# Sliding-window attention and a two-layer MLP on one core: the attention of batches 2 to 7 in blocks of 64 queries and 128 keys

## The chip, the core and the metric

The kernel runs on one core of a Trainium2 chip. A core has a matmul engine (PE, TensorE), three engines for elementwise work (DVE, VectorE; ACT, ScalarE; POOL, GpSimd) and an engine that issues most transfers (SP, SyncE). They run side by side and wait for each other by semaphores; each works through its own instructions in order. Sixteen DMA engines move data. Matmuls write to PSUM, which has eight banks of 512 float32 columns per partition; everything else lies in SBUF. The metric is the time of one execution on the device in microseconds (us).

## The reference

There are 8 batches, 8 heads, 576 tokens and a head dimension of 64. Each query attends to keys at most 32 positions away. The result, 4608 tokens of 512 values, goes through two layers (512 to 2048 to 512) with a leaky ReLU between.

```python
scores = scale * np.matmul(q, k.transpose(0, 1, 3, 2))
mask = np.abs(pos[:, None] - pos[None, :]) <= window      # window = 32
scores = np.where(mask, scores, -1000000000.0)
attn = np.exp(scores - max); attn = attn / (sum + 1e-09)
x = np.matmul(attn, v)          # then (B, S, H*D)
h = x @ w_in; g = np.maximum(0.01 * h, h); out = g @ w_out
```

The kernel leaves the maximum out: the scores are small, so exp is taken directly, masked entries are multiplied by 0, and the products are divided by the sum of the exponentials.

## The kernel before

**Tiling.** Two heads make a pair, which fills the 128 partitions (2 x 64); there are four pairs. The attention of a half batch (288 queries) and one pair is a *chunk*: 8 chunks a batch, 64 in all. The first layer works by *groups* of 288 tokens, 16 of them; for each, `h_tile` makes 16 tiles of 128 hidden units from four matmuls of 288 columns (L348), and ACT evicts each with the leaky ReLU (L355). The second layer works by 36 output tiles of 128 tokens, each 16 matmuls of 512 columns (L390), evicted by ACT (L395) and stored by SP (L396).

**A chunk.** `score` multiplies five block-diagonal key blocks (`kbd`: 64 keys of each head, zeros in the other head's quarter) by windows of queries (L275). Keys 64 at a time with a window of 32 each side reach up to 128 queries, so the five blocks overlap and the scores go to two layers of 288 columns. ACT takes the exponential of 576 columns (L280), POOL multiplies by a mask (L282) into `prob`. `join` adds the two layers on DVE (L292); `sums` multiplies the result by a block of ones, so that each column's sum stands on all 64 rows of its head (L301), and DVE takes the reciprocal (L309). `product` multiplies five block-diagonal value blocks (`vbd`) by `prob` (L320), and DVE's multiply by the reciprocal (L334) writes the columns of `xT`, the first layer's input.

**Getting batches in.** For batches 0 and 1 PE transposes queries and keys (`transposes`, L225). For batches 2 to 7 SP loads q and k in pieces of 512 bytes (L81), POOL casts them to bfloat16, two copies for each (L197), SP issues one DMA transpose each for q and k (`transpose_dma`, L212), and two DVE copies put the keys into `kbd` (`place_keys`, L260). Two tokens lie side by side in a piece, so tokens stand even and odd apart all the way, and the eviction L355 puts them back in order. Values are loaded by head (L91) and cast by POOL into `vbd` (L205; batch 1's by ACT, L203).

**Order.** The order of work on each engine is that of the program. `step()` does one chunk's share: the join of the next chunk, the score of the chunk after the next, sums, product and scaling of this one, placements, casts and loads by tables of due steps (`qk_due`, `v_due`). At the end of the program a list `plan` holds the matmuls of both layers, tile after tile; `spend` walks a clock along it and calls `step()` when the next chunk is due. A group's last chunk is due 4 us (`LEAD`) of the plan's time ahead of its first layer. Batch 0, and the start of batch 1, are written out by hand before that.

**Buffers.** `xT` and `gT` (the hidden units) are rings of 1152 tokens. PSUM has four banks for both layers (`mm`), two for the scores (one set), and one each for `x` and `s`.

Of the kernel before, what the change touches and what calls it, by code (L numbers as in the profile page):

```python
# [16 lines left out]
def kernel(  # L17
# [38 lines left out]
    outp = ctx.enter_context(tc.tile_pool(name="outp", bufs=4))  # L56
# [11 lines left out]
    def load_qk(b, p, behind=None):  # L68
# [3 lines left out]
        for into, src, name in ((qf, q, "qf"), (kf, k, "kf")):  # L72
# [5 lines left out]
            if b < BY_DMA:  # L78
                nc.sync.dma_start(out=t, in_=heads.rearrange("a (p c) d -> p a (c d)", c=RUN))
            else:  # L80
                nc.sync.dma_start(  # L81
                    out=t.rearrange("p a (g e) -> p a g e", g=3),
                    in_=heads.rearrange("a (g p c) d -> p a g (c d)", g=3, c=2),
                )
            into[b, p] = t

    def load_v(b, p):

        t = fload.tile([128, NB, D], FP32, name=f"vf{p}")
# [5 lines left out]
        vf[b, p] = t  # L95
# [24 lines left out]
    kbd = [const.tile([128, NPAIR, NB, 128], BF16, name=f"kbd{i}") for i in range(2)]  # L120
    vbd = [const.tile([128, NPAIR, NB, 128], BF16, name=f"vbd{i}") for i in range(2)]
# [12 lines left out]
    nc.vector.memset(kbd[0], 0.0)  # L134
# [31 lines left out]

    NPROB = 6
# [10 lines left out]
    RING = 4 * HALF  # L178
    xT = const.tile([128, NPAIR, RING], BF16)
# [4 lines left out]
    qT = {}  # L184

    def cast_qk(b, p, q_eng=None):
        for eng, src, dst in ((q_eng or nc.gpsimd, qf, qb), (nc.gpsimd, kf, kb)):
            if b < BY_DMA:
                parts = [(dst[:, p], src[b, p].rearrange("p a (c d) -> p c a d", d=D))]
            else:  # L190
                by_c = src[b, p].rearrange("p a (g c d) -> c p g a d", g=3, c=2)
                parts = [(dst[:, p, 3 * c:3 * c + 3], by_c[c]) for c in range(2)]
            for to, tok in parts:
                if eng is nc.scalar:
                    eng.activation(out=to, in_=tok, func=AF.Copy)
                else:
                    eng.tensor_copy(out=to, in_=tok)  # L197
# [8 lines left out]

    def transpose_dma(b, p):
        if b not in qT:
            qT[b] = attn.tile([128, NPAIR, S], BF16, name="qT")
        kT = kt.tile([128, S], BF16, name="kT")  # L210
        for t, src in ((qT[b][:, p], qb), (kT, kb)):
            nc.sync.dma_start_transpose(  # L212
                out=t.rearrange("p (c i) -> p c i", c=RUN),
                in_=src[:, p].rearrange("p c a d -> p (c a d)"),
            )
        landing.append((8 * (b - 1) + 4 + p, b, p, kT))

    def transposes(b):

        qT[b] = attn.tile([128, NPAIR, S], BF16, name="qT")  # L220
# [27 lines left out]
    def place_keys():  # L248

        while landing and landing[0][0] <= state["done"]:  # L250
            unplaced.append(landing.pop(0)[1:])
        while unplaced:
            b, p, kT = unplaced.pop(0)
            for a in range(2):
                r = slice(64 * a, 64 * a + 64)
                to = kbd[b % 2][r, p, :, r]
                if b < BY_DMA:
                    nc.vector.tensor_copy(out=to, in_=kT[r].rearrange("p (n j) -> p n j", j=64))  # L258
                else:
                    nc.vector.tensor_copy(  # L260
                        out=to.rearrange("p n (m c) -> p n c m", c=2),
                        in_=kT[r].rearrange("p (c n m) -> p n c m", c=2, n=NB),
                    )
# [5 lines left out]

    def score(i):  # L270
        b, hf, p = where(i)
# [23 lines left out]
    def sums(i):  # L295
# [3 lines left out]
        s = xps.tile([128, HALF], FP32, name="s")  # L299
# [12 lines left out]
    def product(i):  # L312
# [3 lines left out]
        x = xps.tile([128, HALF], FP32, name="x")  # L316
# [19 lines left out]
    def weighted(i):  # L336
        if probs[i][2] is None:
            sums(i)
# [6 lines left out]

    def h_mms(g, f, h, cs):
        for c in cs:
            nc.tensor.matmul(  # L348
                h[:, 0:HALF], w_in_bf[:, c, ts(f, 128)], xT[:, c, ds(g * HALF % RING, HALF)],
# [3 lines left out]
    def h_out(g, f, h):  # L353

        nc.scalar.activation(  # L355
            out=gT[:, f, ds(g * HALF % RING, HALF)].rearrange("p (i c) -> p i c", c=2),
# [293 lines left out]
```

## Time and profile before

| | |
|---|---|
| median of three runs | 320.09 us (319.89 to 320.62) |
| span of the profiled execution | 318.99 us |
| PE busy, 0 to 53 us | 39.37 us |
| PE busy, 53 to 122 us | 68.55 of 69 us |
| PE busy, 122 to 250 us | 127.53 of 128 us |
| first layer, L348 | 1024 matmuls of 288 columns |
| second layer, L390 | 16 matmuls for each of 36 tiles |
| reciprocal L309, DVE | 64 times 1956 ns |
| mask L282, POOL | 64 times 1276 ns |
| exp L280, ACT | 64 times 648 ns |
| eviction L355, ACT | 256 times 412 ns |
| waits of DVE's reciprocal on PE's sums L301 | 53.3 us in all |

A row of a group of instructions gives the busy time and the mean of one. Busy times of matmuls overlap, since one starts before the former has left the array; the time that a matmul takes in a row of others is read from start to start. The profiled execution is one of its own, so its span differs a little from the median of the runs. Idle time of an engine that is not the one that sets the end costs nothing.

### The profile page before, as it was taken

To read this page: it belongs to the slowest core of one execution; us is meant where nothing else is said; L and a number is where in the kernel's file an instruction comes from. 1 tells how busy PE (TensorE), PEld (TensorE's weight loads), DVE (VectorE), ACT (ScalarE), POOL (GpSimd) and SP (SyncE) were. 2 spreads that over 40 slices of the span, in tenths; PEclk is the share of its full clock that TensorE was granted. 3 is DMA by queue.
4 is the path that set the end of the run, shared out by engine and by line. 5 is a ranking of instruction groups with operands and counts; after the bars stand their busy time and mean duration, and the time that the engine had idled before them with its cause. 6 is when DMAs were issued, how large, how long until landed. Compare 5 with 4: busy or idle time off the path is not lost.

```text
span 319.0 us, 6455 instructions
## 1 busy us (share of the span) xinstructions
PE 301.1 (94%) x2429; PEld 203.5 (64%) x2449; DVE 220.7 (69%) x258; ACT 183.5 (58%) x394; POOL 191.2 (60%) x251
## 2 busy tenths in 40 slices
PE   2678998999999999999999999999999999999996
PEld 1457764576765858576765858576665858576653
DVE  5688886869755987688755987688745988565100
ACT  7686688574652828375552828465552837464531
POOL 7899963974646866585646866586637866330000
PEclk9999999999999999999999999999999999999999
DMA  8999998997998989399835996399833440000102
GB/s 189 224 184 229 269 242 188 242 200 180 223 245 167 245 148 210 79 237 202 173 76 114 233 229 151 74 215 223 178 76 104 108 71 33 35 35 2 66 31 71
DMA packets 108400, 49.46 MB, mean 155 GB/s; under 512 B 68816, under 2 KB 103888, under 8 KB 108368
## 3 DMA queue, kind: packets, MB, share of 16 engines
q1 hardware_dynamic: 104144, 44.84, 66.0%
q0 software_dynamic: 4224, 4.19, 8.1%
q8 instruction: 19, 0.31, 0.5%
q14 instruction: 13, 0.11, 0.1%
HBM read 36.70 MB, written 9.44 MB: 145 GB/s over the span
## 4 chain that ended last, share of the span: by engine, by line
PE 88%; DVE 5%; ACT 3%; issue 2%; POOL 1%; ACTq 0%; POOLq 0%; DVEq 0%
PE mm L390 38%; PE mm L348 37%; PE x L320 5%; PE ps L275 5%; PE s L301 2%; DVE r L309 2%; DVE qb L197 1%; PE s L304 1%; DVE kbd L258 1%; POOL prob L282 1%; ACT kT L239 1%; PE tp L225 1%; ACT e L280 1%; ACT vbd L203 1%; DVE kbd L134 1%
## 5 line engine op out<-in xcount | busy, mean ns | idle before, releaser
L309 DVE RECIPROCAL r<-s 128x288 f32<-128x288 f32 x64 | 125.2, 1956 | 57.0 <-PE s L301 53.3
L282 POOL TENSOR_TENSOR prob<-e,mask 128x576 bf16<-128x576 bf16 x64 | 81.6, 1276 | 89.2 <-ACT e L280 42.1
L348 PE MATMUL mm<-xT,w_in_bf 128*128 128x288 bf16 x1024 | 134.0, 286 | 0.1
L390 PE MATMUL mm<-w_out_bf,gT 128*128 128x512 bf16 (+2 forms) x572 | 128.7, 373 | 1.1
L355 ACT ACTIVATE gT<-mm 128x288 bf16<-128x288 f32 x256 | 101.2, 412 | 25.6 <-PE mm L348 9.1
L348 PEld LDWEIGHTS <-w_in_bf 128*128 128x128 bf16 x1024 | 98.4, 98 | 24.5 <-issue 0.3
L390 PEld LDWEIGHTS <-gT 128*128 128x128 bf16 x592 | 56.3, 98 | 59.2
L395 ACT ACTIVATE o_sb<-mm 128x512 f32<-128x512 f32 (+2 forms) x37 | 21.7, 585 | 91.8 <-PE mm L390 89.0
L280 ACT ACTIVATE e<-ps 128x576 bf16<-128x576 f32 x64 | 41.5, 648 | 10.6 <-PE ps L275 10.5
L197 POOL CAST kb<-kf 96x384 bf16<-96x384 f32 (+1 forms) x56 | 34.8, 643 | 4.5 <-DMA kf<-in_k_dram 4.3
L205 POOL CAST vbd<-vf 64x576 bf16<-64x576 f32 x50 | 34.7, 694 | 1.5
L334 DVE TENSOR_TENSOR xT<-x,r 128x288 bf16<-128x288 f32 x64 | 29.2, 457 | 7.8 <-PE x L320 1.1
L260 DVE COPY kbd<-kT 64x576 bf16<-64x576 bf16 x48 | 32.3, 674 | 0.6 <-DMA kT<-kb 0.3
L320 PE MATMUL x<-prob,vbd 128*128 128x128 bf16 (+2 forms) x320 | 26.0, 213 | 2.7 <-ACT vbd L203 1.3
L275 PEld LDWEIGHTS <-kbd 128*128 128x128 bf16 x320 | 20.8, 99 | 10.7 <-DVE kbd L258 1.6
L275 PE MATMUL ps<-qT,kbd 128*128 128x128 bf16 (+2 forms) x320 | 26.3, 214 | 1.3 <-DVE kbd L258 0.8
L197 POOL CAST qb<-qf 96x384 bf16<-96x384 f32 x48 | 24.4, 536 | 0.0
L320 PEld LDWEIGHTS <-vbd 128*128 128x128 bf16 x320 | 20.5, 99 | 5.4 <-ACT vbd L203 1.9
L292 DVE TENSOR_TENSOR both<-prob 128x288 bf16<-128x288 bf16 x52 | 20.0, 384 | 0.9
L301 PE MATMUL s<-both,ones_bd 128*128 128x288 bf16 x52 | 14.9, 286 | 0.0
L258 DVE COPY kbd<-kT 64x576 bf16<-64x576 bf16 x16 | 7.1, 446 | 6.2 <-ACT kT L239 6.0
L225 PE MATMUL tp<-ident,qb 96*128 96x96 bf16 x48 | 4.1, 233 | 6.8 <-DVE qb L197 6.8
(43 smaller groups left out, 87.9 us busy)
## 6 DMA issues: line engine op xcount, KB each, us to landing
qf<-in_q_dram SPq DMA_DIRECT2D x32, 288.0 KB, 4.6
kf<-in_k_dram SPq DMA_DIRECT2D x32, 288.0 KB, 5.3
vf<-in_v_dram SPq DMA_DIRECT2D x64, 144.0 KB, 4.4
out_dram<-o_sb SPq DMA_DIRECT2D x35, 256.0 KB, 3.9
w_in_bf<-in_moe_w_in_dram POOLq DMA_DIRECT2D x4, 512.0 KB, 8.2
w_out_bf<-in_moe_w_out_dram POOLq DMA_DIRECT2D x4, 512.0 KB, 16.4
qT<-qb SPq DMA_TRANSPOSE x24, 4.2
kT<-kb SPq DMA_TRANSPOSE x24, 3.1
```

The costliest lines, as they stand in the source:

```text
L197: eng.tensor_copy(out=to, in_=tok)
L205: nc.gpsimd.tensor_copy(out=vbd[b % 2][r, p, :, r], in_=vf[b, p][r])
L260: nc.vector.tensor_copy(out=to.rearrange("p n (m c) -> p n c m", c=2), in_=kT[r].rearrange("p (c n m) -> p n c m", c=2, n=NB),)
L275: nc.tensor.matmul(ps_v[:, n_, :, i0:i0 + n], kbd[b % 2][:, p, blk], by_c[:, :, hf * EVEN + i0:hf * EVEN + i0 + n], start=True, stop=True,)
L280: nc.scalar.activation(out=e, in_=ps[:, P0:P0 + 2 * HALF], func=AF.Exp, scale=scale)
L282: nc.gpsimd.tensor_mul(pr.rearrange("p n c i -> p (n c i)"), e, mask[hf].rearrange("p n c i -> p (n c i)"),)
L309: nc.vector.reciprocal(r, s)
L320: nc.tensor.matmul(x_v[:, :, i0:i0 + n], vbd[b % 2][:, p, blk, :], pr[:, n_, :, i0:i0 + n], start=(blk == parts[0][1]), stop=(blk == parts ...
L334: nc.vector.tensor_mul(place(i), x, r)
L348: nc.tensor.matmul(h[:, 0:HALF], w_in_bf[:, c, ts(f, 128)], xT[:, c, ds(g * HALF % RING, HALF)], start=(c == 0), stop=(c == DMC - 1),)
L355: nc.scalar.activation(out=gT[:, f, ds(g * HALF % RING, HALF)].rearrange("p (i c) -> p i c", c=2), in_=h[:, 0:HALF].rearrange("p (c i) -> ...
L390: nc.tensor.matmul(o[:, lo:hi], gT[:, f, ds(128 * j % RING, 128)], w_out_bf[:, f, lo:hi], start=(f == 0), stop=(f == FFC - 1),)
```

## The change

Batches 0 and 1 are computed as they were. From batch 2 on:

- The 54 blocks of 64 queries (9 a batch) are numbered through. A chunk is four of them (256 queries) and one pair; it may span two batches. There are 14 x 4 = 56 such chunks, the last four with two blocks each.
- A score is one matmul for each block (L354): 128 keys as weights (64 and 32 on each side, `kz`, padded with zeros at the ends of a batch) and 2 x 64 columns of queries, which stand in `qz` once for each head, with zeros on the other head's rows. Exp and mask are over 512 columns; the mask is one band (`band`). The score bank alternates between two.
- A product is two matmuls for each block (L372), one a head, of 64 columns. Its weights are the head's 64 value columns beside 64 columns of ones (`vw`: values, ones, values), so the product and the sum of the exponentials come out of one matmul. `join` and `sums` are gone there. The sums stand on the other head's partitions: two ACT copies bring them over (L379, L380), then come the reciprocal in SBUF (L381) and two multiplies (L385). `x` alternates between two banks.
- q and k are loaded in pieces of 256 bytes, with tokens in order; POOL casts each in one copy. The DMA transpose writes keys straight into `kz`; the two DVE copies are now of the queries, into `qz` (`place_queries`, L298). Values are loaded for two pairs by five transfers in 128-token windows offset by 32 and cast by three POOL copies (`cast_vw`).
- The first layer works by groups of 256, 256, five times 512, and 384 tokens; the rings are used to 1024 tokens. The due steps come from a table of how many chunks each group needs, with a lead of 5 us.
- `qT`, `kbd` and `vbd` share two large tiles with `qz`, `kz` and `vw`, so zeros and ones are written anew by DVE while batches 0 and 1 run (`clear_q`, `ready`, called through `chore`). There are three output buffers instead of four.

```diff
+    def score_blocks(i):
+        p, bs = i % NPAIR, blocks_of(i)
+        n = 2 * 64 * len(bs)
+        lo = 512 * (i % 2)
+        sc = ps[:, lo:lo + n].rearrange("p (a w i) -> p a w i", a=2, i=64)
+        for w, (b, m) in enumerate(bs):
+            nc.tensor.matmul(
+                sc[:, :, w], kz[b % 2][:, p, 64 * m:64 * m + 128],
+                qz[b % 2][:, p, :, 64 * m:64 * m + 64], start=True, stop=True,
+            )
+        e = attn.tile([128, 2 * HALF], BF16, name="e")
+        nc.scalar.activation(out=e[:, 0:n], in_=ps[:, lo:lo + n], func=AF.Exp, scale=scale)
+        pr = prob[:, i % NPROB].rearrange("p n c i -> p (n c i)")[:, 0:n]
+        nc.gpsimd.tensor_mul(pr, e[:, 0:n], band.rearrange("p w i -> p (w i)")[:, 0:n])
...
+    def product_blocks(i):
...
+        x = xps.tile([128, 512], FP32, name="xs"[i % 2])
+        x = x[:, 0:2 * n].rearrange("p (a w i) -> p a w i", a=2, i=64)
+        for a in range(2):
+            for w, (b, m) in enumerate(bs):
+                nc.tensor.matmul(
+                    x[:, a, w],
+                    vw[b % 2][:, p, m, a:a + 2].rearrange("p n d -> p (n d)"),
+                    pr[:, a, w], start=True, stop=True,
+                )
+        x = x.rearrange("p a w i -> p a (w i)")
+        r = recip.tile([128, HALF], FP32, name="r")
+        nc.scalar.activation(out=r[0:64, 0:n], in_=x[64:128, 0], func=AF.Copy)
+        nc.scalar.activation(out=r[64:128, 0:n], in_=x[0:64, 1], func=AF.Copy)
+        nc.vector.reciprocal(r[:, 0:n], r[:, 0:n])
+        t0 = (i - OLD) // NPAIR * 256 % NEW_RING
+        for a in range(2):
+            rows = slice(64 * a, 64 * a + 64)
+            nc.vector.tensor_mul(xT[rows, p, t0:t0 + n], x[rows, a], r[rows, 0:n])
...
+    def place_queries():
+        while landing and landing[0][0] <= state["done"]:
+            _, b, p, t = landing.pop(0)
+            for a in range(2):
+                r = slice(64 * a, 64 * a + 64)
+                nc.vector.tensor_copy(out=qz[b % 2][r, p, a], in_=t[r])
...
+    def clear_q(i):
+        for p in range(NPAIR):
+            for a in range(2):
+                nc.vector.memset(qz[i][64 * (1 - a):64 * (1 - a) + 64, p, a], 0.0)
+                yield
...
+    GROUPS = [(HALF * g, HALF) for g in range(2 * BY_DMA)]
+    t0, new = 0, NTOK - BY_DMA * S
+    while t0 < new:
+        n = 256 if t0 < 512 else min(512, new - t0)
+        GROUPS.append((t0 % NEW_RING, n))
+        t0 += n
...
+    chores.append(clear_q(0))
...
+        if f >= 8:
+            chore()
...
+    need, steps = [], 3 * NPAIR
+    for g in range(3, len(GROUPS)):
+        steps += NPAIR if g < 2 * BY_DMA else NPAIR * -(-GROUPS[g][1] // 256)
+        need.append((at[g] - (LEAD if g < 2 * BY_DMA else 5.0), steps))
+    t = at[2] - LEAD + 1.8
+    while len(due) + 8 < NC:
+        done = len(due) + 8
+        rate, until, count = max(((n - done) / (a - t), a, n) for a, n in need if n > done)
+        due += [t + (i + 1) / rate for i in range(count - done)]
+        t = until
```

In the changed code the first layer's matmul is L477 and its eviction L488, the second layer's matmul L523 and its eviction L528, the exp L359 and the mask multiply L361.

More of the change, by code (lines that the diff above doesn't have):

```diff
@@ L587 @@
         t += us
+    LEAD = 4.0
     due = [O_US * n for n in (4, 7, 10, 12)]
[L589 to L591 removed]
+    need, steps = [], 3 * NPAIR
[8 more added lines that the diff above has]
+        t = until
     clock = 0.0
```

206 lines of the change are left out of this document (142 added, 64 removed).

## The prediction, made before the changed kernel was run

> **What bounds the kernel now.** I read the engine shares and slices of the page first, then the sums over four stretches, then PE's order of time in one stretch of the steady stage.
>
> ```profile
> span 319.0 us, 6455 instructions
> PE 301.1 (94%) x2429; PEld 203.5 (64%) x2449; DVE 220.7 (69%) x258; ACT 183.5 (58%) x394; POOL 191.2 (60%) x251
> PE   2678998999999999999999999999999999999996
> PEclk9999999999999999999999999999999999999999
> ```
>
> ```profile
> core 0: us, PE busy (x) PEld busy (x) DVE busy (x) ACT busy (x) POOL busy (x), PEclk, DMA share, GB/s
> 0.00:53.00 53.00, 39.37 (x384) 29.25 (x386) 40.08 (x47) 40.06 (x76) 41.19 (x53) 1.00 1.10 216
> 53.00:122.00 69.00, 68.55 (x537) 44.86 (x541) 52.70 (x63) 38.76 (x83) 45.56 (x61) 1.00 1.06 209
> 122.00:250.00 128.00, 127.53 (x1014) 85.87 (x1021) 94.01 (x111) 70.42 (x159) 83.92 (x115) 1.00 0.74 159
> ```
>
> ```profile
> 205.05 0.40 PE L320 MATMUL x<-prob,vbd 128*128 128x96 bf16 x5
> 205.29 3.62 PE L390 MATMUL mm<-w_out_bf,gT 128*128 128x512 bf16 x16
> 208.74 0.40 PE L275 MATMUL ps<-qT,kbd 128*128 128x64 bf16 x5
> 208.98 0.29 PE L301 MATMUL s<-both,ones_bd 128*128 128x288 bf16 x1
> 209.10 0.40 PE L320 MATMUL x<-prob,vbd 128*128 128x64 bf16 x5
> 209.34 3.59 PE L348 MATMUL mm<-xT,w_in_bf 128*128 128x288 bf16 x28
> 212.77 0.40 PE L275 MATMUL ps<-qT,kbd 128*128 128x64 bf16 x5
> ```
>
> From 53 us on PE is filled (68.55 of 69, 127.53 of 128), at the full granted clock. A busy time overlaps its neighbour, so I price matmuls by start to start. 16 matmuls of 512 columns: 208.74 - 205.29 = 3.45, 0.216 each. 28 of 288: 212.77 - 209.34 = 3.43, 0.1225 each. Five score blocks, 64+96+3x128 = 544 columns: 0.24. One sum of 288: 0.12. All four fit columns/2400 + 0.0025 us, and I use that. No weight load shows: five new weights went through in 0.24 us. So from 53 us to the end time is the sum of PE's columns, and only before 53 us does PE wait (13.6 us not busy there).
>
> **The sum on PE, batches 2 to 7.** *Removed:* one sum of exponentials per chunk (L301), 48 x 0.1225 = 5.88 us. *Replaced:* a chunk of 288 queries had five score and five product blocks, 0.239 each, 48 x 0.478 = 22.96. After it there are 6 x 9 blocks x 4 head pairs = 216 scores of 2x64 columns at 0.0558 = 12.06, and 432 products of 64 columns at 0.0292 = 12.60, together 24.66: +1.70. *First layer:* 12 groups x 64 x 0.1225 = 94.08 becomes 2 x 64 x 0.1092 + 5 x 64 x 0.2158 + 64 x 0.1625 = 93.44: -0.64. The second layer is unchanged. Sum -5.88 + 1.70 - 0.64 = **-4.82 us**. Nothing hides this: PE has no idle time to put it in.
>
> **The price of a 64-column product.** No row shows eight of them in a row, each with its own weights. From the 0.24 us of a mixed block of five, three of 128 (0.0558) and one of 96 (0.0425) leave 0.030 for the 64. The other end is the weight load's busy time, 98 ns (98.4 us over 1024 loads). I take 0.0292, since the row is the same instruction with a new weight ahead and behind; no gain below it is possible while a column takes 1/2400 us.
>
> [...]
>
> **The other engines in the steady stage.** By PE's columns a chunk comes every 3.91 us after ((2 x 13.81 + 8 x 0.457)/8), 4.50 before ((7.84 + 7.78 + 4 x 0.60)/4). *DVE:* reciprocal 1956 x 256/288 = 1.74, two multiplies 457 x 256/288 = 0.41 each; in four steps of a batch two copies of 64x576 into the zero-padded queries. The join (0.38) goes. The copies have two near rows: 0.446 (L258, unbroken runs of 64) and 0.674 (L260, stride). I take 0.446, as both sides are unbroken; below it 0.25 is conceivable. A loaded step is 3.45 against 1.96 + 0.46 + 0.38 + 1.35 = 4.15 before. *ACT:* exp of 512 about 0.60 (the 512-column eviction L395 took 0.597), and two new copies of 64x256 between 0.277 (128 columns) and 0.412 (288): 0.385, so 1.37 a chunk against 0.65; each 512-wide eviction 0.60 against PE's 0.863. In a first-layer stretch of 16 tiles with four chunks: 9.6 + 5.5 = 15.1 on ACT, 13.8 + 1.8 = 15.6 on PE. Tight, but four PSUM buffers hold 2.6 us, so nothing is added. *POOL:* mask 1.276 x 512/576 = 1.13; casts of q and k 2 x 0.93 (was 2.26); the three value copies of 640, 512 and 512 elements 2.0 by L205's 0.694 for 576 (was 1.39). At most 3.1 of 3.91. *SP and DMA:* q and k come in 256-byte pieces, not 512. The packet records between 45 and 60 us give 19.9 ns for the 256-byte ones (value loads) and 39.2 for the 512-byte ones: twice the packets at half the price, 0. The dear end is 29.4 ns (256-byte ones of the first 30 us): +1.4 us of all engines for each q and k pair. Ten value issues replace eight in a batch.
>
> In the order of issue, the first matmul that needs a group's last chunk stands 4.19 us of columns behind that chunk's product before, 6.07 after; the chain in it (ACT copies 0.8, reciprocal 1.74, multiplies 0.81) is 3.4. So the steady stage costs nothing extra.
>
> **Where I add time: 42 to 53 us.** Eight clears of 64x288 (qz) stand on DVE among the key placements of batch 1. L134's 1978 ns for 2304 words and L112's 112 for 64 put one at 0.25 to 0.45; I take 0.30, so 1.2 us ahead of each of two placements.
>
> ```profile
> 44.94 0.89 DVE L258 COPY kbd<-kT 64x576 bf16<-64x576 bf16 x2
> 45.86 2.11 DVE L197 CAST qb<-qf 96x768 bf16<-96x768 f32 x1
> 47.89 0.90 DVE L258 COPY kbd<-kT 64x576 bf16<-64x576 bf16 x2
> ```
>
> ```profile
> 46.46 0.40 PE L275 MATMUL ps<-qT,kbd 128*128 128x96 bf16 x5
> 48.42 0.42 PE L225 MATMUL tp<-ident,qb 96*128 96x96 bf16 x6
> 51.54 0.41 PE L320 MATMUL x<-prob,vbd 128*128 128x96 bf16 x5 [1.09 <-ACT vbd L203]
> ```
>
> The score at 46.46 needs the copies that ended at 45.83: 0.63 us of cover, so +0.6. The cast that ended at 47.97 then ends at 49.2, for transposes that would start at 49.0: +0.3. The second four delay the next score by some 0.5, and the 1.09 us wait on ACT at 51.54 takes that up. Taken: **+0.9**; ends 0 and 2.4 (no cover).
>
> **57 to 110 us (steps 12 to 24).** The planner lets chunks come every 3.05 to 3.9 us here to get ahead of the first 512-token group, while DVE still has the rest of the clears and ones (some 20 small fills, about 6 us at 0.86 ns a word), and two batches are placed. DVE's work from step 12 to 23, with the rows above, is some 40 us against PE's 37.4: it falls 2 to 3 us behind, and the waits of scores on placed queries leave 5.6 to 6.7 us behind the product where the chain with a placement takes 4.5 to 6. DMA is at a share of 1.06 there already and gets less time per batch (26 us of PE's columns from step 16 to 24, 37 before). I take **+0.9**; ends 0 and 5.3 (third rival).
>
> **Sum:** 318.99 (span) - 4.82 + 0.9 + 0.9 = 315.97. The median of the runs shown is 320.09, 1.10 above the span; so **317.1 us**.
>
> **Rivals.** *1. 64-column products pay for their weights* (slower). Place: L372. If a load can't be hidden behind 64 columns, a product takes more than 0.0292; at the 128-column spacing of 0.0558 it is 432 x 0.0266 = +11.5, 328.6 us; at 98 ns +29.7. It decides from (4.82 - 1.8)/432 = 7 ns more each. Against it: the 0.030 above; for it: never seen eight times running. *2. The early stage turns on DVE and DMA* (slower). Copies at 0.674: 16 x 0.228 = 3.6, of which some 1 us is covered, 2.6; and the dear 256-byte price, four pairs x 1.4 = 5.6 less some 2.9 of slack between landing and placement, 2.7. With 5.3 in place of 0.9: 321.5. It decides from 3.9 us of stall. For it: the share of 1.06; DVE's L260 waited 0.3 us for a transpose already. Against: the placed queries are the first of the two transposes, and queries are cast in one piece. *3. ACT blocks PE in the groups of 256 and 288 tokens.* There a tile is 0.437 us and the buffers hold 1.3 us against a burst of 0.91 a chunk: three groups at 0.6: 318.9. Against: the eviction of 0.60 at L395 was followed by the exp 0.50 after its start, so ACT gives more than its busy times say. *4. The matmuls removed were hidden anyway*: 320.1. It needs idle time on PE, which is not there.
>
> **How the numbers follow.** Forecast 0.60 (own range 315.3 to 319.0), rival 1 0.10, rival 2 0.17 (319 to 323: faster 0.02, same 0.05, slower 0.10), rival 3 0.05, rival 4 0.03, slower for something not named 0.05. About 0.2% (0.64 us) is what a measurement of this kernel can tell from no change. Faster 0.60 + 0.05 + 0.02 = 0.67; same 0.05 + 0.03 = 0.08; slower 0.10 + 0.10 + 0.05 = 0.25. The range runs from both additions at nothing, less the runs' spread, 314.9, to past rival 2, 322.5; outside lie rival 1 and a little of the rest.
>
> **What would show it.** L372's products start 29 ns apart, L354's 56, L477's 216; PE without idle time from about 110 us on; DVE's loaded steps under 3.9 us. Wrong: idle PE before L372 in every chunk (rival 1), scores L354 waiting on DVE or DMA before 110 us over 4 us in total (rival 2), L477 waiting on ACT (rival 3).

## The result: 327.54 us, slower

| kernel | median us (lowest to highest) | ratio to before, 95% interval | span of the profiled execution |
|---|---|---|---|
| before | 320.10 (319.89 to 320.62) | | 318.99 |
| after | 327.54 (326.79 to 327.91) | 1.0229 [1.0214, 1.0244] | 325.85 |

The profiled execution of after took 327.55 us itself. Its page (the span, the busy times, PE's slices, the granted clock, and the chain that ended last by engine):

```profile
span 325.9 us, 6374 instructions
PE 299.8 (92%) x2282; PEld 177.1 (54%) x2313; DVE 228.2 (70%) x314; ACT 214.1 (66%) x450; POOL 198.0 (61%) x242
PE   2679998999997779999999999999999999999995
PEclk9999999999999799999999999999999999999999
PE 65%; DMA 13%; DVE 8%; POOL 5%; issue 4%; ACT 3%; POOLq 0%; ACTq 0%; DVEq 0%; SPq 0%
```

The same chain in before:

```profile
PE 88%; DVE 5%; ACT 3%; issue 2%; POOL 1%; ACTq 0%; POOLq 0%; DVEq 0%
```

Before, PE's row was all nines behind the eighth slice. Now three slices between 98 and 122 us are sevens, the clock has a seven in the second of them, and transfers hold 13% of the chain that ends last, where they had no part before. The sums over the same two stretches as in the prediction:

```profile
core 0: us, PE busy (x) PEld busy (x) DVE busy (x) ACT busy (x) POOL busy (x), PEclk, DMA share, GB/s
53.00:122.00 69.00, 60.77 (x507) 40.11 (x511) 55.64 (x84) 41.17 (x95) 50.06 (x62) 0.98 1.10 194
122.00:250.00 128.00, 126.55 (x932) 68.94 (x947) 101.14 (x130) 90.42 (x192) 88.30 (x106) 1.00 0.89 168
```

So the loss lies between 53 and 122 us: 60.77 us of PE where before had 68.55. The DMA engines are as busy as they were (1.10 and 1.06) and move less (194 GB/s and 209).

Start to start, PE's columns take 291.0 us against 295.8 before: the predicted 4.82 us are there. The steady stage shows them, here PE in order of time:

```profile
204.32 0.39 PE L354 MATMUL ps<-set 128*128 128x128 bf16 x4
204.54 0.40 PE L372 MATMUL s<-prob,set 128*128 128x64 bf16 x8
204.78 3.62 PE L523 MATMUL mm<-w_out_bf,gT 128*128 128x512 bf16 x16
```

Four scores in 0.22 us and eight products in 0.24: 55 and 30 ns each.

From 57 us on, gaps of over 0.1 us between the end of one matmul's columns and the next start, with a stretch at half the clock, add up to 12.07 us, 0.30 before. That gives -4.82 + 11.77 = 6.95; the span grew by 6.86. (Three smaller terms all but cancel: PE waits 0.6 us less before 57 us, loses 0.3 more in gaps under 0.1 us, and the end behind PE's last matmul is 0.2 longer.) PE's order of time shows where most of it stands (in brackets: the idle time ahead, and what ended it):

```profile
98.26 3.62 PE L523 MATMUL mm<-w_out_bf,gT 128*128 128x512 bf16 x15
101.72 0.22 PE L354 MATMUL ps<-set 128*128 128x128 bf16 x1
104.32 0.34 PE L354 MATMUL ps<-set 128*128 128x128 bf16 x3 [2.38 <-DMA set<-kb]
104.49 0.40 PE L372 MATMUL x<-prob,set 128*128 128x64 bf16 x8
104.73 2.75 PE L523 MATMUL mm<-w_out_bf,gT 128*128 128x512 bf16 x12
107.32 0.22 PE L354 MATMUL ps<-set 128*128 128x128 bf16 x1
109.67 0.37 PE L354 MATMUL ps<-set 128*128 128x128 bf16 x3 [2.13 <-DVE set L298]
109.83 0.63 PE L372 MATMUL s<-prob,set 128*128 128x64 bf16 x8
110.28 4.22 PE L477 MATMUL mm<-xT,w_in_bf 128*128 128x256 bf16 x24
114.34 0.39 PE L354 MATMUL ps<-set 128*128 128x128 bf16 x4
```

A chunk's first block still belongs to batch 2 and starts; the other three belong to batch 3, whose transposed keys and placed queries aren't there. Measured from the end of one matmul's columns to the next start, the gaps are 2.54 us at 101.7, 2.29 at 107.3, 2.24 at 118.0 and 0.56 at 149.1, in all 7.6. Then the 24 matmuls of 256 at 110.28 take 4.06 us to the next line's start, and 24 x 0.1092 = 2.62 would do: 13 of them stand 213 ns apart, half the clock, which costs 1.4. Before that, at 72 to 81 us, four gaps of 0.39 to 0.56 us (1.8 in all) wait for DVE's reciprocals and multiplies. At the tiles of 256 and 288 columns (L477), four gaps of 0.13 to 0.33 us wait for evictions: 0.7. Together 11.5 us, 4.7 of them behind 110 us.

Why batch 3 comes late is read from SP's own queue (second column: how long the issue held it), first after, then before:

```profile
87.41 1.43 SPq L81 DMA_DIRECT2D kf<-in_k_dram  x1
88.94 3.86 SPq L110 DMA_DIRECT2D vbuf<-in_v_dram  x5
...
95.44 2.19 SPq L529 DMA_DIRECT2D out_dram<-o_sb  x1
97.73 2.60 SPq L110 DMA_DIRECT2D vbuf<-in_v_dram  x5
100.44 1.20 SPq L284 DMA_TRANSPOSE kT<-qb  x1
101.75 1.20 SPq L284 DMA_TRANSPOSE set<-kb  x1
...
104.32 1.58 SPq L284 DMA_TRANSPOSE kT<-qb  x1
```

```profile
91.81 3.66 SPq L91 DMA_DIRECT2D vf<-in_v_dram  x4
96.89 1.51 SPq L212 DMA_TRANSPOSE qT<-qb  x1
98.51 1.20 SPq L212 DMA_TRANSPOSE kT<-kb  x1
```

POOL had cast the queries of this transpose in time:

```profile
90.07 0.82 POOL L264 CAST qb<-qf 96x768 bf16<-96x768 f32 x1
```

The cast ended at 90.9, the transpose was issued at 100.44. In those 9.5 us SP worked through the loads and stores that stand ahead of it. An issue took 0.43 to 0.58 us where nothing held it (L81 at 93.50 and at 103.62), so some 6 us of this is issuing (an estimate, twelve issues at 0.5, eight of them of values) and the rest is issues held up, as by 2.19 us at 95.44. In before the queue was empty from 95.5 to 96.89: SP waited for the cast. The packet records say what filled the queue. In before, from 50 to 95.5 us, 9.89 MB went out, among them 9216 packets of 512 bytes at 38.3 ns. In after, from 50 to 100.4, it was 9.87 MB, with all q and k in 256-byte packets, at 23.4 ns. Two of those take 46.8 ns: 9216 x 8.5 ns / 16 engines = 4.9 us, as much as the later end. But that the price makes this end is not shown by the sum: the packets of all kinds took 50.9 us of the 16 engines in before and 53.1 in after, only 2.2 more, since the 256-byte packets of before had taken 26.2 ns. A run shows it instead: with 512-byte pieces and nothing else changed (e2 below) the first transpose of batch 2 is issued at 58.36, 61.21 in after, and that of batch 3 at 94.41, 6.0 us earlier.

### The profile page after: what moved, and what is told of

Read it like the earlier page. It is cut to its first block, busy times and chain, and to the rows that moved or that the text cites. A ratio compares the mean times of both kernels' runs of the same rounds, so it can differ in the third digit from the quotient of the medians.

```text
span 325.9 us, 6374 instructions
## 1 busy us (share of the span) xinstructions
PE 299.8 (92%) x2282; PEld 177.1 (54%) x2313; DVE 228.2 (70%) x314; ACT 214.1 (66%) x450; POOL 198.0 (61%) x242
## 4 chain that ended last, share of the span: by engine, by line
PE 65%; DMA 13%; DVE 8%; POOL 5%; issue 4%; ACT 3%; POOLq 0%; ACTq 0%; DVEq 0%; SPq 0%
PE mm L523 29%; PE mm L477 28%; DMA vbuf<-in_v_dram 5%; DMA kT<-qb 4%; PE ps L354 3%; DVE r L428 3%; DMA qf<-in_q_dram 2%; DVE set L298 2%; PE s L372 2%; PE x L372 2%; DMA set<-kb 1%; POOL qb L264 1%; POOL prob L401 1%; POOL kb L264 1%; ACT e L359 1%
## 5 line engine op out<-in xcount | busy, mean ns | idle before, releaser
L477 PE MATMUL mm<-xT,w_in_bf 128*128 128x512 bf16 (+3 forms) x758 | 134.5, 328 | 0.8 <-ACT gT L488 0.2
L523 PE MATMUL mm<-w_out_bf,gT 128*128 128x512 bf16 (+2 forms) x571 | 128.9, 373 | 1.2
L381 DVE RECIPROCAL r<-r 128x256 f32<-128x256 f32 (+1 forms) x56 | 95.0, 1696 | 36.2 <-ACT r L380 35.6
L361 POOL TENSOR_TENSOR prob<-e,band 128x512 bf16<-128x512 bf16 (+1 forms) x56 | 62.9, 1123 | 77.0 <-ACT e L359 74.0
L488 ACT ACTIVATE gT<-mm 128x512 bf16<-128x512 f32 (+3 forms) x192 | 87.7, 494 | 19.3 <-PE mm L477 15.7
L477 PEld LDWEIGHTS <-w_in_bf 128*128 128x128 bf16 x768 | 73.5, 99 | 46.3 <-issue 0.8
L523 PEld LDWEIGHTS <-gT 128*128 128x128 bf16 x592 | 55.1, 98 | 58.2
L359 ACT ACTIVATE e<-ps 128x512 bf16<-128x512 f32 (+1 forms) x56 | 32.5, 580 | 49.1 <-PE ps L354 41.5
L528 ACT ACTIVATE o_sb<-mm 128x512 f32<-128x512 f32 (+2 forms) x37 | 21.7, 585 | 26.5 <-PE mm L523 21.6
L428 DVE RECIPROCAL r<-s 128x288 f32<-128x288 f32 x16 | 31.2, 1951 | 3.9 <-PE s L423 3.3
L264 POOL CAST kb<-kf 96x768 bf16<-96x768 f32 x32 | 27.8, 870 | 3.9 <-DMA kf<-in_k_dram 3.7
L298 DVE COPY set<-kT 64x576 bf16<-64x576 bf16 x48 | 22.4, 467 | 9.5 <-DMA kT<-qb 8.7
L354 PE MATMUL ps<-set 128*128 128x128 bf16 x216 | 21.9, 219 | 7.0 <-DMA set<-kb 4.5
L354 PEld LDWEIGHTS <-set 128*128 128x128 bf16 x216 | 16.7, 98 | 19.5 <-DMA set<-kb 7.4
L385 DVE TENSOR_TENSOR xT<-s,r 64x256 bf16<-64x256 f32 (+1 forms) x56 | 23.1, 413 | 3.6 <-DVE r L381 0.5
L385 DVE TENSOR_TENSOR xT<-x,r 64x256 bf16<-64x256 f32 (+1 forms) x56 | 23.1, 413 | 3.3
L401 POOL TENSOR_TENSOR prob<-e,mask 128x576 bf16<-128x576 bf16 x16 | 20.3, 1274 | 8.3 <-ACT e L399 7.9
L372 PEld LDWEIGHTS <-set 128*128 128x128 bf16 x432 | 18.2, 99 | 1.0 <-issue 0.5
L278 POOL CAST set<-vbuf 64x512 bf16<-64x512 f32 x24 | 14.6, 610 | 1.5
L279 POOL CAST set<-vbuf 64x512 bf16<-64x512 f32 x24 | 14.6, 608 | 1.2
```

What stands on the lines that cost most here:

```text
L298: nc.vector.tensor_copy(out=qz[b % 2][r, p, a], in_=t[r])
L354: nc.tensor.matmul(sc[:, :, w], kz[b % 2][:, p, 64 * m:64 * m + 128], qz[b % 2][:, p, :, 64 * m:64 * m + 64], start=True, stop=True,)
L359: nc.scalar.activation(out=e[:, 0:n], in_=ps[:, lo:lo + n], func=AF.Exp, scale=scale)
L361: nc.gpsimd.tensor_mul(pr, e[:, 0:n], band.rearrange("p w i -> p (w i)")[:, 0:n])
L372: nc.tensor.matmul(x[:, a, w], vw[b % 2][:, p, m, a:a + 2].rearrange("p n d -> p (n d)"), pr[:, a, w], start=True, stop=True,)
L381: nc.vector.reciprocal(r[:, 0:n], r[:, 0:n])
```

## The experiments

Two theories stood first: *pieces* (q and k in 256-byte pieces make transfers late) and *pace* (the first group of 512 tokens makes the planner ask for steps 16 to 24 every 3.3 us, 4.6 before, sooner than batch 3 can come). In the table, the ratio is to before as measured beside each set of runs (its median went from 320.0 to 320.7 us), and gaps are PE's gaps of over 0.1 us and its stretches at half the clock behind 57 us in the profiled execution. Two slips in the texts on record: where f1, f3 and f5 say batches 2 to 5, it is 2 to 7 (in f6 too), and f6's copies are 24.

| run | median us | ratio, 95% interval | gaps us |
|---|---|---|---|
| after | 327.54 | 1.0229 [1.0214, 1.0244] | 12.1 |
| e1_groups256 | 322.89 | 1.0080 [1.0055, 1.0105] | 6.8 |
| e2_pieces512 | 322.14 | 1.0054 [1.0030, 1.0079] | 6.0 |
| e3_groups256_pieces512 | 321.50 | 1.0061 [1.0040, 1.0083] | 5.4 |
| e4_groups256_to_1024 | 325.29 | 1.0156 [1.0118, 1.0194] | 9.1 |
| x1_q1536 | 333.02 | 1.0418 [1.0388, 1.0447] | 17.6 |
| x2_ones_on_act | 328.12 | 1.0250 [1.0235, 1.0265] | 12.7 |
| c1_q1536_ones | 332.39 | 1.0371 [1.0344, 1.0399] | 15.9 |
| x3_qk1536 | 322.09 | 1.0059 [1.0037, 1.0081] | 6.0 |
| d1_qk1536_nojoin | 321.15 | 1.0014 [0.9992, 1.0036] | 4.0 |
| d2_groups256_split | 320.41 | 0.9998 [0.9980, 1.0015] | 4.0 |
| d3_groups256_split_nojoin | 320.02 | 0.9992 [0.9975, 1.0008] | 2.8 |
| d4_before_pieces256 | 323.71 | 1.0105 [1.0069, 1.0141] | 4.7 |
| f1_all_four | 317.82 | 0.9920 [0.9903, 0.9938] | 1.1 |
| f2_split_nojoin | 327.27 | 1.0213 [1.0188, 1.0239] | 11.9 |
| f3_qk1536_split_nojoin | 319.86 | 0.9997 [0.9980, 1.0015] | 4.0 |
| f4_split_nojoin_v_later | 331.22 | 1.0336 [1.0304, 1.0369] | 13.1 |
| f5_q512_in_order | 318.87 | 0.9940 [0.9920, 0.9960] | 1.1 |
| f6_qk512_in_order | 327.74 | 1.0233 [1.0209, 1.0257] | 10.8 |

### Pieces or pace: e1 to e4

```diff
# e1: groups of 256 throughout; e4: the same up to token 1024
-        n = 256 if t0 < 512 else min(512, new - t0)
+        n = min(256, new - t0)
# e2: two tokens to a piece; e3: both
-                    out=t.rearrange("p a (c d) -> p a c d", d=D),
-                    in_=heads.rearrange("a (c p) d -> p a c d", p=96),
+                    out=t.rearrange("p a (g e) -> p a g e", g=3),
+                    in_=heads.rearrange("a (g p c) d -> p a g (c d)", g=3, c=2),
```

> The changed kernel with every group of the new part at 256 tokens (the last 128), so the planner lets a chunk come every 3.9 us throughout instead of every 3.3 us in steps 16 to 24. Pace theory (the stalls between 70 and 120 us come from the planner running ahead of the transfers): PE's columns cost 0.9 us more, but the 11.7 us of stalls go down to under 2, so 315.5 to 318 us. Pieces theory (q and k in pieces of 256 bytes keep SP's queue behind, whatever the pace): at least half of the stalls stay, 321 us or more.

> The changed kernel, its q and k loaded in pieces of 512 bytes as before the change (same bytes, same tiles; the tokens of batches 2 to 7 then stand in another order, so the output is not the reference's). Pieces theory: 9216 packets of 38 ns instead of 18432 of 23.4 ns between 50 and 100 us free about 5 us of all DMA engines, the first transposes of batch 3 leave SP 5 us earlier, and most stalls go: 316 to 319.5 us. Pace theory: the stalls stay above 5 us, 322 us or more.

> Both edits together (tokens in another order, as in the run with 512-byte pieces). Both theories: no stall of over 1 us after 60 us, about 315.5 to 317 us. If stalls of several us remain, a third cause stands behind them (DVE's fills, or the value loads of two pairs standing ahead of the transposes in SP's order).

> The changed kernel with groups of 256 up to token 1024 of the new part, 512 after it: the lead for the first 512-token group is gathered over twice as many steps (3.6 us a chunk, 16 to 24, instead of 3.3). Pace theory: stalls between those of the changed kernel and of 256 throughout, 316 to 321 us. Pieces theory: little better than the changed kernel, 323 us or more.

Either edit takes about 5 us out, and neither theory alone gives the number it expected. With the slower pace (e1) 1.3 and 0.3 us of waits on batch 3 are left at 114 to 119 us; with larger pieces (e2) no wait on a transfer is left, but 1.7, 0.7 and 0.2 us at 105 to 114 where a score waits for DVE's placed queries. Both together (e3) leave no wait on batch 3 at all, and yet 321.5 in place of 315.5 to 317: a third cause. PE in order of time in e3 shows it:

```profile
134.86 1.91 PE L477 MATMUL mm<-xT,w_in_bf 128*128 128x256 bf16 x16
136.94 1.47 PE L477 MATMUL mm<-xT,w_in_bf 128*128 128x256 bf16 x12 [0.17 <-ACT gT L488]
```

Sixteen matmuls of 256 need 1.75 us, and the next starts 2.08 behind the first: 0.33 us lost, and 0.13 more in most groups. ACT does an exp of 512 columns and two copies in a row, 1.4 us, while the four PSUM buffers hold 1.3 us of such tiles by the prediction's count. That is the third rival of the prediction, for 13 groups and not three; e1 loses 4.3 us to it. e4, in between in pace, has 325.29 and something left of every cause.

### ACT's burst taken apart: d2

```diff
# in step(); rest() is weighted(i), place_keys(), place_queries();
# spend() calls it when the clock has got there
-        weighted(i)
+        if i >= OLD:
+            late.append(clock + 0.8)
+        else:
+            rest()
```

> The run with 256-token groups throughout (322.9 us), with a chunk's products, copies and scaling placed 0.8 us of the plan later than its score, so that ACT has the exp and the two copies apart. ACT-burst theory (in a 256-token group the exp and the copies together hold the evictions back longer than four PSUM buffers cover, 0.46 us a group in 13 groups): 317.5 to 319.5 us. If ACT is short of time altogether: within 0.7 us of 322.9.

This is e1 with the copies 0.8 us of the plan behind the exp. The waits on L488 are gone, all of them:

```profile
130.06 0.39 PE L354 MATMUL ps<-set 128*128 128x128 bf16 x4
130.28 0.60 PE L477 MATMUL mm<-xT,w_in_bf 128*128 128x256 bf16 x4
130.72 1.03 PE L523 MATMUL mm<-w_out_bf,gT 128*128 128x512 bf16 x4
131.58 0.40 PE L372 MATMUL s<-prob,set 128*128 128x64 bf16 x8
```

The products now stand apart from the scores, and no bracket is left. 2.5 us came back. At least 3.4 had been expected: the waits on batch 3 are longer now (0.84, 0.98, 1.02 us).

### DVE's lag at 72 to 81 us: x2, x3, d1

```diff
# x2: the ones of vw written by ACT, not by DVE's memsets
# x3: e2 with pieces of 1536 bytes (six tokens), for q and k; d1: x3 and
-    JOINED = 12
+    JOINED = 99
```

> The changed kernel with the fills of ones (four of 128x576 a set) moved from DVE to ACT. DVE-lag theory: the four waits of products on DVE between 72 and 82 us (about 1.9 us in all) go, and a little more: 325 to 326.5 us. Transfers-only theory: the time stays within 327 to 328 us, since the transposes are as late as before.

> The changed kernel at its own pace, queries and keys both loaded in pieces of 1536 bytes (same bytes; the tokens of batches 2 to 7 stand in another order inside a batch, queries and keys alike, so the scores are of other tokens). Pieces theory: 5.8 us less of all DMA engines a batch; the waits on transposes between 100 and 120 us go altogether and with them the throttled stretch behind them: 317.5 to 320.5 us, what stays being DVE's 2 us and ACT's 0.6. Pace theory: over 3 us of the waits on transposes stay, 322 us or more.

> The run with queries and keys in pieces of 1536 bytes (322.1 us; tokens in another order), with the joins of chunks 12 to 15 taken off DVE (PE sums the two layers by two matmuls instead, +0.5 us of columns). DVE-lag theory: DVE gets 1.8 us back in steps 11 to 15, the 2.0 us of waits of PE between 72 and 83 us go and the 2.6 us between 104 and 116 shrink: 319 to 321 us. If those waits have another cause (POOL's or ACT's lateness), the time rises by the 0.5 us: 322 us or more.

x2 is no faster than after, and the waits at 75 to 82 us are still there (2.1 us): the fills that it takes from DVE aren't what is late. x3 repeats e2 to 0.1 us, so 512 bytes are enough. At after's own pace larger pieces alone take the waits on transfers away; x3's time still falls into the range of the pace theory, because 2.8 us behind placed queries and DVE's lag stay. d1 leaves out the joins of chunks 12 to 15 (DVE adds two layers to spare PE a sum of 0.12 us each), and the gaps at 72 to 83 us (2.0 in x3) are gone. It is 0.9 us faster than x3, although PE has 0.5 us more of columns. With DVE that full, the join costs more than the sum that it saves.

### The pieces alone, in the kernel before: d4

```diff
# open/before's load for batches 2 to 7
-  pieces of two tokens
+  pieces of one token (256 bytes), "a (c p) d -> p a c d"
```

> The kernel before, its q and k of batches 2 to 7 loaded in pieces of 256 bytes (tokens in another order), nothing else. If the pieces cost time by themselves: 322 us or more. If they need the faster pace to matter (at the old pace batch 3 is placed about 8 us after its transposes could be issued): 320 to 321 us.

323.71, 3.6 us above before: the pieces cost time by themselves, without the faster pace. PE in order of time:

```profile
119.31 0.40 PE L275 MATMUL ps<-qT,kbd 128*128 128x96 bf16 x5
121.47 0.28 PE L301 MATMUL s<-both,ones_bd 128*128 128x288 bf16 x1 [1.76 <-DVE r L309]
122.04 0.40 PE L320 MATMUL x<-prob,vbd 128*128 128x96 bf16 x5 [0.28 <-DVE xT L334]
122.27 5.26 PE L348 MATMUL mm<-xT,w_in_bf 128*128 128x288 bf16 x28
127.38 0.40 PE L275 MATMUL ps<-qT,kbd 128*128 128x96 bf16 x5
```

The first transposes of batch 3 are issued at 100.03 (96.89 before), DVE waits for the keys and is late with the next reciprocal: 1.92, 0.36 and 0.44 us. The 28 matmuls of 288 then take 5.1 us where the same line took 3.43 before: the half clock again. It belongs to this execution, which took 324.50; three others, at a granted clock of 1.000, took 323.07 to 323.72, so the 3.6 us doesn't come from it.

### The order of tokens put back by DVE: x1, c1

```diff
# x1: q alone in 1536-byte pieces
-                nc.vector.tensor_copy(out=qz[b % 2][r, p, a], in_=t[r])
+                nc.vector.tensor_copy(
+                    out=qz[b % 2][r, p, a].rearrange("p (i c) -> p i c", c=RUN),
+                    in_=t[r].rearrange("p (c i) -> p i c", c=RUN))
```

> The changed kernel with the queries of batches 2 to 7 loaded in pieces of 1536 bytes (six tokens of a head beside each other) and put into token order by the two DVE copies into qz, which then read with a stride; keys as they were. Pieces theory: the q loads fall from 4608 packets of 23.4 ns to 768 of about 80 ns a batch, 2.9 us less of all DMA engines, so more than a third of the 7.6 us of waits on transposes goes: 321 to 325 us. If DVE decides instead: the copies grow from 0.47 to about 0.67 us each and the time does not fall, 327 us or more.

> Both edits. If the waits on transposes and the lag of DVE are separate terms, their gains add: 319 to 323.5 us. If each only moves the other's wait, it is no better than the better one of the two.

Worse than after, by the second branch. The same group of DVE's copies in after and in x1 (busy us, mean ns | idle before):

```profile
L298 DVE COPY set<-kT 64x576 bf16<-64x576 bf16 x48 | 22.4, 467 | 9.5 <-DMA kT<-qb 8.7
```

```profile
L298 DVE COPY set<-kT 64x576 bf16<-64x576 bf16 x48 | 46.3, 965 | 1.0
```

24 us more on DVE, and in x1 the scores wait 7.4 us for L298. A copy took 965 ns where 0.67 us had been expected (the last section has more on that). c1, with the ones on ACT as well, is 0.6 us lower with an interval that overlaps x1's, and slower than x2 alone: the second branch here too.

### What is left, and all at once: d3, f1, f2, f3, f4

```diff
# d3: d2 and JOINED = 99; f1: d3 and 1536-byte pieces
# f2: d3 with after's groups; f3: f2 and 1536-byte pieces
# f4: d3, and the loads of the next batch's values four steps later
+        for b, p in v_due.get(i - 4, ()):
+            if b + 1 < B and p % 2 == 1:
+                load_v_pairs(b + 1, p - 1)
```

> The same without the joins of chunks 12 to 15. At this pace DVE's lag costs 0.6 us and PE's added columns 0.5: within 0.7 us of the run before it by the DVE-lag theory; over 1 us faster if DVE's lag also makes the 1.6 us of late scores at 114 to 120 us.

> Every cause found so far taken away at once: groups of 256, the copies and scaling of a step 0.8 us of the plan behind its score, no joins for batches 2 on, and queries and keys of batches 2 to 5 in 1536-byte pieces, whose tokens stand in another order in the blocks, so that the output is another one. If the 2.2 us of waits that d3_groups256_split_nojoin keeps at 109, 115 and 119 us are the price of the pieces, they go: span 315.5 to 316.2, time 317 to 318. If they belong to the pace or to the placing, they stay: time 319.5 to 320.5.

> The changed kernel with its own groups of 512 and its own pieces, but with the copies and scaling of a step behind its score and no joins: takes 2.0 us of DVE's lag and 0.6 us of ACT's bursts out of 327.5. If the waits on transfers are a third cause by themselves, they stay at 7 to 9 us: time 324.5 to 326. If they follow from the lag of the steps before, the time falls under 322.

> As f2_split_nojoin with queries and keys of batches 2 to 5 in 1536-byte pieces (another order of the tokens, another output), so the changed kernel's own pace with nothing else left. If the 2.7 us of waits behind placed queries at 105 to 114 us that x3 and d1 keep are the price of the pace, they stay: time 320 to 321 (319 in the runs without the stall at 44 to 46 us). If they came from ACT's bursts, time 317 to 318.

> d3_groups256_split_nojoin with the loads of the next batch's values issued four steps later, so behind the first two transposes of that batch on SP's queue instead of ahead of them; the output is the reference's. If the queue's order is what makes the transposes late, up to 2.2 us of waits go: time 318 to 319. If the bytes themselves are, the transposes are no earlier or the values are late instead: 320 to 322.

d3 is level with before (0.9992): 2.2 us of waits on batch 3 are left and hold back the gain. f1 takes those but for 0.5 us, and its page reads as the prediction had it:

```profile
span 316.2 us, 7239 instructions
PE   2688998999999999999999999999999999999995
PEclk9999999999999999999999999999999999999999
```

316.2 us of span where the forecast had 315.97, 317.82 us of time where it had 317.1, and 0.992 of before with an interval that leaves no doubt. With the four causes taken away 1.1 us of gaps are left of 12.1. That the spans meet to 0.3 us is partly luck: in place of the forecast's two additions of 0.9 us f1 pays 1.45 us of columns that the forecast hadn't (1.0 for groups of 256, 0.5 for the sums by two matmuls) and 0.8 of gaps. f2 shows that at after's own pace the waits on transfers aren't a consequence of the other two: 327.27, 1.3 us over what was expected. DVE's lag and ACT's bursts are gone, but the steps now run ahead to the first wait on batch 3:

```profile
99.98 0.22 PE L354 MATMUL ps<-set 128*128 128x128 bf16 x1
104.12 0.50 PE L354 MATMUL ps<-set 128*128 128x128 bf16 x3 [3.92 <-DMA set<-kb]
104.41 1.91 PE L523 MATMUL mm<-w_out_bf,gT 128*128 128x512 bf16 x4
```

That gap is 4.08 us from the end of the first matmul's columns. The waits on batch 3 aren't longer in all (7.3 us, 7.1 in after up to 120 us), but the stretches at half the clock now cost 3.8 us in place of 1.4: four matmuls of 512 columns in 1.7 us, where 0.86 would do. f3 against f2 is the price of the pieces at that pace, 7.4 us; the waits behind placed queries stay, 3.3 us in all with a longest gap of 1.75, so they are the price of the pace, not of ACT's bursts.

f4 is far slower, 331.22, where at most 322 had been expected. The transposes do go out sooner (94.33, 100.04 in d3), so the order in SP's queue is part of what makes them late. But now the values are late, and POOL, which works in order, stands still for them:

```profile
POOL set L277 <- DMA vbuf<-in_v_dram: 29.7, 6, 7.9
```

29.7 us in six waits (the longest 7.9), while masks and casts are queued behind. Turning the queue round moves the wait; larger pieces take it away.

### The price had back in the reference's order: f5, f6

```diff
# f5: d3 with q in 512-byte pieces; 64 queries stand evens first
-                sc[:, :, w], kz[b % 2][:, p, 64 * m:64 * m + 128],
-                qz[b % 2][:, p, :, 64 * m:64 * m + 64], start=True, stop=True,
+                sc[:, :, w].rearrange("p a (e i) -> p a e i", e=2), kz[...],
+                qz[b % 2][:, p].rearrange("p a (g e i) -> p a g e i", g=3, e=2)[
+                    :, :, m // 3, :, 32 * (m % 3):32 * (m % 3) + 32],
# the band by pattern=[[0, 8], [-1, 2], [-2, 32]], and in h_out
+            to = to.rearrange("p (w i e) -> p w e i", i=32, e=2)
+            h = h.rearrange("p (w e i) -> p w e i", i=32, e=2)
# f6: k in 512-byte pieces too, transposed into a buffer, then
+            nc.vector.tensor_copy(
+                out=kz[b % 2][:, p, W:W + S].rearrange("q (g i e) -> q g e i", g=3, e=2),
+                in_=u.rearrange("q (g e i) -> q g e i", g=3, e=2))
```

> A version that computes the reference: d3_groups256_split_nojoin with the queries of batches 2 to 5 in 512-byte pieces of two tokens. A block's 64 queries stand evens first in the moving side, the band is made in that order, and ACT's Prelu puts the tokens right as it does for batches 0 and 1, so no copy is added. If the pieces are the price, half of it goes: 1 us or more of d3's 2.2 us of waits, time 318 to 319.2. If the half that is left (keys) is what comes late, or ACT's strided reads block PE, 319.5 to 321.

> As f5_q512_in_order, with the keys in 512-byte pieces too; their transposes land in a buffer, and one DVE copy per pair and batch puts them into the set in token order (16 copies of 128x576, near 1 us each by x1_q1536). If DVE has the room, as f1_all_four: time 317.5 to 318.5. If the copies make DVE late as in x1_q1536: over 320.

f5 is the version that beats both kernels: 318.87 us, 0.994 of before [0.992, 0.996]. Half of the small packets are gone at no copy, the first transposes go out at 97.24, and of the waits on batch 3 one of 0.52 us is left. ACT's reordering read costs nothing (L488's form of 256 columns has the same mean in d3 and f5, 387 ns). f6 pays 24 copies on an engine that is full:

```profile
L308 DVE COPY set<-kU 128x576 bf16<-128x576 bf16 x24 | 19.2, 800 | 0.7
```

19.2 us more on DVE, and scores wait for placed sets from 105 us to 271.

## Why the prediction was wrong

**What held.** The price list on PE: -4.82 us of columns, with products 30 ns apart and scores 55. The new rows on the other engines are near their estimates too: exp 0.595 us (0.60), copies on ACT 0.38 (0.385), reciprocal 1.75 (1.74), mask 1.16 (1.13). The first rival (products that pay for weights) falls, and so does the fourth (removed work that was hidden): f1, with the stalls taken away, is 2.4 us faster than before (317.82 and 320.25 measured side by side).

**42 to 53 us, +0.9.** One landmark is in both traces, a gap of 0.30 us in batch 1: at 60.5 us before and at 59.9 in after. The 0.6 isn't the change's: d4, whose early code is before's, has it at 59.9 too. The profiled executions fall into two kinds. In one PE doesn't wait at 44 us (after, d3, d4, e1 to e3, f1 and others). In the other it waits 0.7 to 0.8 us there for DVE's cast of batch 1's queries (before, d1, d2, f5 and others), and then the changed code waits another 0.99 at 46.4 us, behind clears that now stand between cast and placement: the landmark is at 61.6 to 61.7 in d2 and f5, 1.1 later than in before. So the term is 0 in one kind and 1.1 in the other, within the ends that were given, and it was a choice between two cases and not one size. What decides between them stands in the last section.

**57 to 110 us, +0.9: the step that failed.** The step measured 11.8 in place of 0.9: 7.0 up to 110 us and 4.7 behind it, where PE was to have no idle time. The mechanism is the second rival's, and it was mis-sized in three places.

1. *"Twice the packets at half the price, 0."* The 19.9 ns came from value loads at 45 to 60 us. The same records of before give 26.1 ns at 60 to 80 us and 29.4 at 80 to 100, where the change puts half of its own packets, against 37.0 and 38.1 for 512 bytes: in traffic a packet cost much more than half. After's own, 23.4, makes a pair of q and k 2304 x 23.4 / 16 - 1152 x 38.3 / 16 = 0.6 us dearer. That is under the dear end of 1.4, but eight pairs stand ahead of batch 3's first transposes in SP's queue and the rival counted four: 4.9 us by these prices, and 6.0 by e2's queue, of which 2.9 are there when batch 2's transposes go out. The rival's 5.6 before slack was near that because its price was too high and its count too low, which is luck; the forecast itself had 0.
2. *The pace was seen and given no price.* The step says that steps 16 to 24 get 26 us in place of 37, and then uses a slack of 2.9 us that belongs to the old pace. Batch 3's scores are wanted at 101.7 us, when its first transpose has just been issued. e1 (pace back, pieces kept) and e2 (pieces back, pace kept) each return about 5 us; d4 shows that the pieces cost 3.6 us by themselves.
3. *What follows from a wait.* That DVE falls 2 to 3 us behind was seen, but only scores on placed queries were to pay for it; the products of the last old chunks paid 1.8 us at 72 to 81, by the joins (d1). The half clock behind the gaps takes 1.4 us in the trace and was no term. What it adds to the time is open: the one execution of after with a granted clock of 1.000 took 327.91 us, no less than the three at 0.993 to 0.995 (326.79 to 327.55), but the wait at 44 us, which comes and goes, is worth as much.

In after 512 bytes in two packets take 46.8 ns (2 x 23.4), in before 38.3 ns in one. That is a factor of 1.22, where the step's "half the price" has 1.

**The third rival** was right in place and near in size: 0.33 and 0.13 us, together 0.46, in a group of 256, for 0.6 predicted. In after it is small, since only its few narrow groups feel it; it hides the gain wherever one slows the pace by narrow groups.

**The range** ended at 322.5 because rival 2 was priced on its own. Its parts aren't independent: larger packets shorten the wait, a slower pace hides it, and after, which has small pieces and a fast pace at once, has 7.6 us of waits on batch 3 where the rival had 5.3.

## What to carry to other kernels

Take the price of a transfer from records of the stretch where the changed transfers will stand, and count every transfer that is queued ahead of the one that matters, not only its own. When a change lets the planned steps come faster, work out anew when each input is wanted: slack that was read from the old pace is gone. An operation that adds a burst to an engine between the bound engine's evictions should be put apart from the next burst, which here was worth 2.5 us (d2 against e1) and added no instruction.

## What the hardware showed that I had not expected

**Half the clock behind short gaps.** In f2 a gap of 4.08 us at 100.0 has half the clock behind it: the next 512-column matmuls stand 427 ns apart. Shorter gaps did it too. In after 13 matmuls of 256 columns stand 213 ns apart from 110.5 us on, behind a gap of 2.29 us (at 107.3); in d4, 13 of 288 columns lose 0.118 us each behind 0.36, 1.92 and 0.44. Yet behind gaps of 2.54 (at 101.7) and 2.24 us (at 118.0) the matmuls of after go on at full speed.

The traces' own records of the granted clock tell more. Up to the last matmul it is at 0.5 of full speed in stretches of 3.41 us (one of twice that, in f2): at 109.81 in after, 122.76 in d4, 111.80 in x1, 110.60 in e4, 103.13 and 120.19 in f2, 128.55 and 166.10 in f4. These six executions have a mean granted clock of 0.984 to 0.995, the 14 others 0.998 to 1.000. In each trace the stretches begin a whole number of 3.41 us after the clock first became full (in after at 17.66, and 109.81 is 27 times 3.413 us later), so each trace can be counted out from there in cells of that length. PE's idle time in these cells, over all 20 traces, separates the two cases. In the cells ahead of these eight stretches PE was idle for 0.64 to 0.92 of the cell. No other cell comes above 0.61 (x2, 116.51 to 119.92). So in these traces it is not the length of a gap that tells the two cases apart but the idle share of one cell: at least 0.64 ahead of a stretch at half the clock, at most 0.61 elsewhere. Why is not shown. In after the 2.29 us lie in one cell (0.67), the 2.54 are cut in two (0.36 and 0.39), and of the 2.24 only 2.0 lie in one (0.60). One stretch doesn't fit: in f2 the clock stays at half for a second cell, though PE was idle for only 0.29 of the first.

**DVE's copies wait for POOL.** L298 in after takes 292 to 307 ns in the 19 cases in which POOL runs nothing beside it, and 575 on average, up to 1220, in the 29 in which it does. These 29 are of two kinds. In 11 the copy starts first: 292 to 308 ns. In 18 an instruction of POOL is already running: 391 to 1220, each time what was left of that instruction and some 165 ns more. The prediction's 446 ns was near the mean (467) of two quite different numbers, which is luck. What makes a copy wait for POOL is not shown. x1's strided copies wait in the same way (635 to 647 ns where POOL runs nothing as they start, 642 to 1627 where it does); f6's strided copies of 128x576, 792 to 809 ns with POOL beside them and 793 without, show no sign of it.

The wait at 44 us has the same pattern. DVE casts the queries of a pair of batch 1 there and POOL the keys, and whichever starts first decides. In d2 POOL is ahead by 0.02 us, in after DVE by 0.3:

```profile
41.90 0.83 POOL L264 CAST kb<-kf 96x768 bf16<-96x768 f32 x1 [2.19 <-DMA kf<-in_k_dram]
41.92 3.21 DVE L264 CAST qb<-qf 96x768 bf16<-96x768 f32 x1
```

```profile
42.03 0.56 DVE L264 CAST qb<-qf 96x768 bf16<-96x768 f32 x1
```

In the 8 traces in which POOL starts first, DVE's cast takes 3.1 to 3.2 us, over POOL's cast and the two fills behind it; in 11 of the 12 in which DVE starts first, it takes 0.56 (c1, with 1.5, is the other). Executions of one kernel seem to differ by this wait too: six of e3 took 321.3 to 321.6 us and three 323.2 to 323.3. Differences of 1 us between medians of a few runs are to be read with that in mind.
